# Fifth group's preparation moved half a unit and more back, and head 13 loaded in half rows and transposed by VectorE

## The chip, the core and the metric

The kernel runs on one core of a Trainium2 chip. Its engines are TensorE (PE; the weight loads of its matmuls are listed apart as PEld), VectorE (DVE), ScalarE (ACT), GpSimd (POOL) and SyncE (SP), which here only issues transfers. Each takes its instructions in program order and waits on semaphores for what the others produce. DMA transfers are issued from SP and from POOL and run on 16 DMA engines. The metric is the device time of one launch in microseconds, as the median of several runs.

## What is computed

Routed attention over 4 batches and 8 heads of 768 tokens with 64 dimensions each, and then a gated feed-forward layer (512 to 1536 and back) on the 3072 rows that come out. A query sees only the keys whose nearest of 16 centroids is the same as its own:

```python
q_assign = np.argmax(np.einsum('bhsd,hcd->bhsc', q_n, c_n), axis=-1)
k_assign = np.argmax(np.einsum('bhsd,hcd->bhsc', k_n, c_n), axis=-1)
mask = q_assign[:, :, :, None] == k_assign[:, :, None, :]
scores = np.where(mask, scale * np.matmul(q, k.transpose(0, 1, 3, 2)), -1e9)
attn = softmax(scores); x = attn @ v          # rows of all heads side by side
xn = x / sqrt(mean(x * x) + 1e-6) * rms_g
out = (silu(xn @ w_gate) * (xn @ w_val)) @ w_out
```

## The kernel before

**Units and groups.** A unit is half a batch's queries (384) for all 8 heads; there are 8 units, u = 0 to 7, and units 2b and 2b+1 belong to batch b. A group is four heads of one batch; there are 8 groups, g = 0 to 7, and head n (0 to 31) of the whole job lies in group n // 4. Units 4 and 5 use groups 4 and 5: group 4, "the fifth", is first needed at the start of unit 4, group 5 in its middle.

**What a unit does.** `attention` walks through 24 gaps, three for each head. In each gap TensorE makes two score matmuls (`s`, L348), ScalarE takes their exponential into `pT` (L352), and once per head TensorE multiplies the head before by its values into `acc` (`pv`, L366). After each pair of heads VectorE divides by the sums (`inv` L371, `x` L373), and that frees the one `acc` buffer. The mask is not applied as a mask: a one-hot of the cluster, 16 rows long, is put under the 64 rows of each transposed query and key (`qext`, `kext`), scaled so that other clusters vanish in the exponential.

**What fills the gaps.** `attention` also takes a list `fill` of pairs of a weight and a piece of work, and hands them out so that the sum of weights keeps step with the gaps. For u of 2 and more, and g = u + 2, the list is: the last 8 of the 24 gate and value parts (`gv`, L444) of the feed-forward layer of unit u-2; `rms(u-1)`, the norm of the unit before; some loads of queries and keys; the 9 output parts `o` of unit u-2 (`out_mm`, L469: 4 matmuls, three parts to a tile of 128 rows, the third followed by a copy on ScalarE and a store from SP, L473); and the first 16 gate and value parts of unit u-1. Between the last two kinds the preparation of group g is spread: `rows`, and then `clusters`.

**The preparation of a group** (`group_work`). For each head: `trans` of the queries and of the keys; then `both`, which casts both halves of the queries and one half of the keys (`cast`, L240), casts the head's v (`vcast`, L243) and issues from SP the v load of head n+4 and the query and key loads of head n+6 (`others`); then a cast of the other half of the keys. These are the 16 `rows`. `clusters` are: the products with the centroids (`sc`, L254; 16 matmuls), on VectorE a transpose, a maximum, a comparison and a transpose back for queries and keys each (L257, L262, L266, L286, with a scaling at L285 for the keys), and 16 small DMAs issued from POOL that put the one-hots under `qext` and `kext` (`place`, L297).

**Two kinds of head.** For n < BH = 14 a head is loaded with one DMA of 192 KB for the queries and one for the keys (L88), TensorE transposes it in float32 (`tq`, L221), and ScalarE or VectorE evicts it (L227, L225); the key casts are VectorE's. For n of 14 and more it is loaded in half rows of 32 floats, four DMAs of 48 KB each for queries and for keys (L96), so that VectorE's transpose in blocks of 32 (L217) gives the same layout with no TensorE and no PSUM; the key casts are POOL's. In unit 1, group 3 (heads 12 to 15) is prepared after group 2's cluster steps; heads 12 and 13 are of the first kind there. Its casts on POOL have the three loads of `wo` woven in (`load_o`, L207, with a cast from float32 in the transfer). `second_batch`, in unit 0, issues the loads of heads 12 and 13 and of v8 to v11.

**Loads held back.** LATE lists heads whose query and key loads are not issued in `others` but in a unit's fill after `rms`: 19, 20 and 21 in unit 2, 24 and 25 in unit 3, 28 and 29 in unit 4. `rms` ends with a transposing DMA from SP (L406) that makes `xnT`, which the gate and value parts of the same unit read.

**Buffers that matter.** Six staging buffers hold queries and keys (a load of head n waits until head n-6 is transposed), eight hold v, three hold pairs of transposed heads (`qkT`), and three PSUM banks (`ps_g`) serve all of `gen`: gate, val, o, sc and tq.

Of the kernel before, what the change touches and what calls it, by code (L numbers as in the profile page):

```python
# [22 lines left out]
def kernel(  # L23
# [13 lines left out]
    B, H, S, D = q.shape  # L37
# [7 lines left out]
    HG = 4  # L45
# [8 lines left out]
    CUT = 2 * FC - 8  # L54
    LEAD = 6
    NQ, NV = 6, 8
    AV = 4
    LATE = [19] + [n for n in range(20, B * H) if n % HG < 2]
    BH = 14
    BG = BH // HG  # L60

    ctx.enter_context(tc.manual_schedule())
# [17 lines left out]
    def src(a, n):  # L80
        b, h = divmod(n, H)
        return a[b, h].rearrange("(p t) d -> p t d", t=ST)

    def load(n, part, on=None):
        if n not in staged:
            staged[n] = stage.tile([P, 2, ST, D], F32, tag="qk", name="qk")
        if n < BH:
            (on or nc.sync).dma_start(out=staged[n][:, part], in_=src((q, k)[part], n))  # L88
            return

        to = staged[n][:, part].rearrange("p t d -> p (t d)").rearrange("p (i r d) -> p i r d", i=HT, d=32)
        of = (q, k)[part][n // H, n % H].rearrange("(r p i e) (c d) -> e c p i r d", p=32, i=HT, e=2, d=32)
        for e in range(2):
            for c in range(2):
                r = 32 * (2 * e + c)
                nc.sync.dma_start(out=to[r:r + 32], in_=of[e, c])  # L96

    def load_qk(n):
        if n < B * H:
            load(n, 0)  # L100
            load(n, 1)

    def load_v(n, vq=None):
        if n >= B * H:
            return
        stagedv[n] = stage.tile([P, ST, D], F32, tag="vs", name="vs", bufs=NV)
        (vq or nc.sync).dma_start(out=stagedv[n], in_=src(v, n))
# [104 lines left out]
    def trans(g, h, part, on=None):  # L212
        if (g, h // 2) not in qkT:
            qkT[g, h // 2] = qk32.tile([P, 2, 2, UQ], F32, tag="qkT", name="qkT")
        qk = staged[g * HG + h]
        if g * HG + h >= BH:
            nc.vector.transpose(qkT[g, h // 2][:, h % 2, part], qk[:, part].rearrange("p t d -> p (t d)"))  # L217
            return
        ps = ps_g.tile([P, UQ], F32, tag="gen", name="tq")
        for i in range(HT):  # L220
            nc.tensor.transpose(ps[:, i * P:(i + 1) * P], qk[:, part, 2 * i:2 * i + 2].rearrange("p t d -> p (t d)"),  # L221
                                ident_f)
        to, by = qkT[g, h // 2][:, h % 2, part], 1.0 / ZS if part and g < BG else 1.0
        if on is nc.vector:
            nc.vector.tensor_scalar_mul(to, ps, by)  # L225
        else:
            nc.scalar.activation(to, ps, ACT.Copy, scale=by)  # L227
# [5 lines left out]
    def cast(on, g, h, part, es=(0, 1)):  # L233
        for e in es:
            to = cols((kext if part else qext)[g % 4][:D, h], g, e)
            of = qkT[g, h // 2][e * D:(e + 1) * D, h % 2, part]
            if on is nc.scalar:
                nc.scalar.copy(to, of)
            else:
                on.tensor_copy(to, of)  # L240

    def vcast(n):
        nc.gpsimd.tensor_copy(vbf[n // HG % 4][:, n % HG, :, :D], stagedv[n])  # L243
# [24 lines left out]
    def cluster_steps(g, m):  # L268

        of = {}  # L270

        def products():
            of["cl"] = cluster_products(g, [(h, m) for h in range(HG)])

        def most():
            of["mx"] = largest(of["cl"])

        def same():
            of["ohT"] = asg.tile([P, UQ], BF16, tag="ohT", name="ohT", bufs=2)
            compare(of["ohT"].rearrange("p (b e c) -> p b e c", e=2, c=NC), of["cl"], of["mx"])  # L280

        def back():
            put[g, m] = asg.tile([P, UQ], BF16, tag="oh", name="oh", bufs=3)
            if m and g >= BG:
                nc.vector.tensor_scalar_mul(of["ohT"], of["ohT"], ZS)  # L285
            nc.vector.transpose(put[g, m], of["ohT"])  # L286

        return [products, most, same, back]
# [3 lines left out]
    def place(on, g, m, es=(0, 1)):  # L292

        ext = (kext if m else qext)[g % 4]
        for h in range(HG):
            for e in es:
                on.dma_start(out=ext[D:D + NC, h, e * UQ:(e + 1) * UQ],  # L297
                             in_=put[g, m][32 * h + e * NC:32 * h + (e + 1) * NC])
# [190 lines left out]
    def group_work(g):  # L489

        t, c = [], []
        for h in range(HG):
            n = g * HG + h
            w = 0.0 if n >= BH else 0.3
            t += [(w, lambda h=h: trans(g, h, 0)), (w, lambda h=h: trans(g, h, 1))]

            def others(n=n):
                vcast(n)
                load_v(n + AV)
                if n + NQ not in LATE:  # L500
                    load_qk(n + NQ)

            def both(h=h, f=others):
                cast(nc.gpsimd, g, h, 0)
                f()
                cast(nc.gpsimd if g * HG + h >= BH else nc.vector, g, h, 1, (0,))
            if g == 2:
                c.append((0.0, others))
            else:
                c += [(0.0, both), (0.0, lambda h=h: cast(nc.gpsimd if g * HG + h >= BH else nc.vector, g, h, 1, (1,)))]  # L510
        a = []
        for m in range(2):
            a += [(0.0 if i else 0.7, f) for i, f in enumerate(cluster_steps(g, m))]
            if g == 3:
                a.append((0.0, lambda m=m: place(nc.gpsimd, g, m)))
            elif g == 2:
                a.append((0.0, (lambda: (place(nc.gpsimd, g, 1), place(nc.gpsimd, g, 0, (1,)))) if m else
                          (lambda: place(nc.gpsimd, g, 0, (0,)))))
        if g > 3:
            a[:1] = [(1.4, lambda f=(a[0][1], a.pop(4)[1]): [x() for x in f])]  # L520
            a.append((0.0, lambda: [place(nc.gpsimd, g, m) for m in range(2)]))
        return t, c, a
# [12 lines left out]
    def spread(a, b):  # L535

        if not a:
            return list(b)
        w, n = [], 0
        for i, x in enumerate(a):  # L540
            w.append(x)
            while n < len(b) * (i + 1) // len(a):
                w.append(b[n])
                n += 1
        return w

    def ffn_work(u):
        n = UNITS[u][2] / HT
        return [(0.64 * n, lambda f=f, val=val: gv(u, f, val)) for f in range(FC) for val in (False, True)]

    def out_work(u):
        return [(0.86, lambda t=t, p=p: out_mm(u, t, p)) for t in range(UNITS[u][2]) for p in range(3)]
# [127 lines left out]
    for u in range(1, NU):  # L680
        ffn, o, g = ffn_work(u - 1), out_work(u - 2) if u > 1 else [], u + 2
        if u == 1:
            t, c, a = group_work(2)
            t3, c3, a3 = group_work(3)
            n = LEAD - 4
            o3 = [(0.0, lambda i=i: load_o(i)) for i in range(0, FC, 4)]
            prep = c + a + spread(weave(t3[n:], c3), o3) + a3[:5]
            idle = const.tile([P, 1], BF16)

            def norm():  # L690
                rms(0)
                nc.gpsimd.tensor_copy(idle, xn[0][:, CC - 1, HT - 1, P - 1:])
                for h in range(HG):
                    casts(pool_, H + h, K0, Q0, K1, Q1)

            hooks = {(1, 0, 0): late[6], (1, 0, 1): lambda: (late[7](), norm())}
            hooks.update({(1, *divmod(2 + i, HT)): t3[i][1] for i in range(n)})
            hooks[1, *divmod(LEAD - 1, HT)] = lambda: xtrans_all(0)
            fill = spread(ffn[:CUT], prep)
            attention([(1, h) for h in range(H)], fill, LEAD, hooks)  # L700
        else:
            fill = ffn_work(u - 2)[CUT:]
            if u == 2:
                fill = fill[:1] + spread(fill[1:], [(0.0, f) for _, f in a3[5:]])
            fill.append((0.0, lambda u=u: rms(u - 1)))
            rows, clusters = group(g)
            fill += [(0.0, lambda n=n: load_qk(n)) for n in LATE if n - n % HG == (u + 3) * HG or (u, n) == (2, 19)]
            n = 12 if u == 2 else len(rows)
            fill += spread(o, rows[:n]) + spread(ffn[:CUT], [(0.0, f) for _, f in rows[n:]] + clusters)
            attention([(u, h) for h in range(H)], fill, 1 if g < NG else 0, ahead=1)  # L710
    rest = ffn_work(NU - 2)[CUT:]
    rest[0][1]()
# [39 lines left out]
```

## Time and profile before

| | us |
|---|---|
| median of five runs | 328.94 |
| the five runs | 328.22 to 329.5 |
| the profiled execution | 329.44 |
| its span in the trace | 327.7 |
| VectorE busy, of 7.94 us from 104.34 to 112.28 (last gate and value parts, unit 3) | 5.51 |
| the same, of 7.37 us from 112.28 to 119.65 (output parts, unit 3) | 6.47 |
| DMA share from 28 to 44 us, and from 61 to 78 us | 1.29 and 1.09 |

The page gives for each engine the time that it was busy and its share of the span. A group is all instructions of one line, engine, operation and tile, as "out<-in", with the count, the total and the mean. The waits list who stood idle until whom: total, times, longest. A timeline row has start, duration, engine, line, operation, tiles, count, and in brackets the idle time before it with what ended it. The chain of waits follows the execution back from its last instruction to what released each step. A DMA share of 1 is 16 engines all busy[...].

### The profile page before, as it was taken

The page shows a single profiled execution, that of the slowest core. Times are in us where ns is not written, and L with a number is a line of the kernel's source. Part 1 is how long each engine was busy: PE and PEld are TensorE (multiplying, and loading weights), DVE is VectorE, ACT ScalarE, POOL GpSimd, SP SyncE. Part 2 cuts the span into 40 slices and gives each one's busy share as a digit, 9 for nine tenths or more (in the row PEclk, how much of TensorE's full clock was granted, in tenths as well). Part 3 has the DMA queues.
Part 4 walks back from the last instruction along what each step waited for, and adds up shares of the span by engine and source line. Part 5 has one row for each costly group of instructions (what it writes and reads, how often), then busy time and mean ns, then how long its engine had stood idle before and what let it go on. Part 6 is the DMA issues. An engine that isn't in the chain of part 4 may idle for free.

```text
span 327.7 us, 7794 instructions
## 1 busy us (share of the span) xinstructions
PE 318.7 (97%) x2851; PEld 191.4 (58%) x2865; DVE 222.8 (68%) x509; ACT 245.8 (75%) x425; POOL 137.6 (42%) x277
## 2 busy tenths in 40 slices
PE   8999899998999999999999999999999999999996
PEld 4546656654556555665566555665566656655654
DVE  6999978879378785877678694876265644685430
ACT  5899988976778867897778877798779868863322
POOL 5999499985935356450926347350000000000000
PEclk9999999999999999999999999999999999999999
DMA  7999995797546644561646540000700040001002
GB/s 261 331 268 259 239 156 103 128 184 166 91 71 159 139 88 72 117 153 60 103 85 132 142 114 34 6 21 1 146 3 0 2 112 34 0 2 74 25 1 96
DMA packets 88742, 34.24 MB, mean 104 GB/s; under 512 B 70400, under 2 KB 85632, under 8 KB 88704
## 3 DMA queue, kind: packets, MB, share of 16 engines
q1 hardware_dynamic: 79536, 27.45, 35.2%
q0 software_dynamic: 8880, 5.91, 11.1%
q8 instruction: 22, 0.36, 0.5%
q10 hardware_dynamic: 288, 0.39, 0.4%
q14 instruction: 16, 0.13, 0.1%
HBM read 28.61 MB, written 6.29 MB: 107 GB/s over the span
## 4 chain that ended last, share of the span: by engine, by line
PE 78%; DVE 9%; POOL 4%; DMA 4%; ACT 2%; issue 2%; DVEq 0%; ACTq 0%
PE o L469 18%; PE gate L444 17%; PE val L444 16%; PE s L348 15%; PE acc L366 8%; DMA wo<-in_moe_w_out_dram 3%; PE sc L254 2%; POOL qext L240 1%; POOL kext L297 1%; DVE kext L332 1%; DVE qext L332 1%; DVE pads L327 1%; DMA boot<-in_centroids_dram 1%; DVE x L373 1%; PE o L480 1%
## 5 line engine op out<-in xcount | busy, mean ns | idle before, releaser
L352 ACT ACTIVATE pT<-s,off 128x768 bf16<-128x768 f32 x192 | 170.9, 904 | 30.9 <-PE s L348 30.2
L348 PE MATMUL s<-qext,kext 80*128 80x384 bf16 x384 | 94.8, 327 | 1.5 <-ACT pT L352 0.8
L444 PE MATMUL gate<-xnT,wg 128*128 128x384 bf16 x384 | 78.3, 325 | 0.1
L444 PE MATMUL val<-xnT,wv 128*128 128x384 bf16 x384 | 78.1, 326 | 0.0
L453 DVE SCALAR_TENSOR_TENSOR th<-th,gate 128x384 f32<-128x384 f32 x84 | 46.2, 551 | 34.8 <-ACT th L452 34.2
L469 PE MATMUL o<-wo,gvT 128*128 128x512 bf16 x262 | 66.3, 378 | 2.0 <-DMA wo<-in_moe_w_out_dram 1.3
L348 PEld LDWEIGHTS <-kext 80*128 80x128 bf16 x384 | 36.4, 98 | 35.0 <-issue 7.4
L452 ACT ACTIVATE th<-gate 128x384 f32<-128x384 f32 x84 | 41.2, 490 | 15.3 <-PE gate L444 14.5
L457 DVE SCALAR_TENSOR_TENSOR gvT<-th,val 128x384 bf16<-128x384 f32 x84 | 46.2, 550 | 9.3 <-PE val L444 3.4
L444 PEld LDWEIGHTS <-wg 128*128 128x128 bf16 x384 | 36.1, 97 | 23.4 <-issue 0.8
L366 PEld LDWEIGHTS <-pT 128*128 128x128 bf16 x1152 | 43.4, 97 | 10.1 <-DVE x L373 1.1
L444 PEld LDWEIGHTS <-wv 128*128 128x128 bf16 x384 | 35.6, 97 | 22.5 <-issue 0.6
L240 POOL CAST qext<-qkT 64x384 bf16<-64x384 f32 x64 | 35.3, 557 | 29.6 <-DVE inv L371 17.5
L366 PE MATMUL acc<-vbf,pT 128*128 128x65 bf16 x1152 | 45.7, 193 | 0.6 <-ACT pT L352 0.2
L469 PEld LDWEIGHTS <-gvT 128*128 128x128 bf16 x276 | 25.9, 97 | 26.9 <-issue 1.4
L297 POOL DMA_DIRECT2D qext<-oh x48 | 23.1, 492 | 33.9 <-DVE oh L286 29.2
L240 POOL CAST kext<-qkT 64x384 bf16<-64x384 f32 x58 | 31.4, 542 | 4.4 <-DVE qkT L225 2.5
L297 POOL DMA_DIRECT2D kext<-oh x48 | 23.1, 488 | 8.3 <-DVE oh L286 7.1
L472 ACT COPY o_sb<-o 128x512 f32<-128x512 f32 x23 | 13.5, 585 | 17.3 <-PE o L469 17.3
L371 DVE RECIPROCAL inv<-acc 128x6 f32<-128x6 f32 x32 | 6.0, 188 | 25.1 <-PE acc L366 24.7
L373 DVE TENSOR_TENSOR x<-acc,inv 128x384 f32<-128x384 f32 x32 | 17.8, 558 | 1.1
L217 DVE STREAM_TRANSPOSE qkT<-qk 128x384 f32<-128x384 f32 x36 | 18.1, 550 | 0.0
(83 smaller groups left out, 228.7 us busy)
## 6 DMA issues: line engine op xcount, KB each, us to landing
vs<-in_v_dram SPq DMA_DIRECT2D x32, 192.0 KB, 4.4
out_dram<-o_sb SPq DMA_DIRECT2D x23, 256.0 KB, 2.5
qk<-in_q_dram SPq DMA_DIRECT2D x72, 48.0 KB, 2.8
qk<-in_k_dram SPq DMA_DIRECT2D x72, 48.0 KB, 2.5
qk<-in_q_dram SPq DMA_DIRECT2D x14, 192.0 KB, 4.9
qk<-in_k_dram SPq DMA_DIRECT2D x12, 192.0 KB, 5.1
wg<-in_moe_w_gate_dram POOLq DMA_DIRECT2D x4, 384.0 KB, 8.0
wv<-in_moe_w_val_dram POOLq DMA_DIRECT2D x4, 384.0 KB, 9.6
```

What stands on the lines that cost most here:

```text
L217: nc.vector.transpose(qkT[g, h // 2][:, h % 2, part], qk[:, part].rearrange("p t d -> p (t d)"))
L240: on.tensor_copy(to, of)
L297: on.dma_start(out=ext[D:D + NC, h, e * UQ:(e + 1) * UQ], in_=put[g, m][32 * h + e * NC:32 * h + (e + 1) * NC])
L348: nc.tensor.matmul(ps[:, j, :w] if nt == HT else flat[:, j * w:(j + 1) * w], lhsT=cols(kext[g % 4][:KR, hh], g, kc // HT, kc % HT * P, (kc ...
L352: nc.scalar.activation(pT[u, h][:, n * i:n * i + n, :w], of, ACT.Exp, bias=off, scale=scale if g >= BG else scale * ZS)
L366: nc.tensor.matmul(acc[:, h % 2, t], lhsT=pT[u, h][:, kc, t * P:(t + 1) * P], rhs=vbf[g % 4][:, hh, kc % HT * 2 + kc // HT], start=kc == 0 ...
L373: nc.vector.tensor_tensor(dst, acc[:, :, :nt, :D], inv[:, :, :nt].unsqueeze(3).broadcast_to([P, 2, nt, D]), op=ALU.mult)
L444: nc.tensor.matmul(ps, lhsT=w[:, c, f * P:(f + 1) * P], rhs=xnT[u][:, c, :n], start=c == 0, stop=c == CC - 1)
L452: nc.scalar.activation(th, ps, ACT.Tanh, scale=0.5)
L453: nc.vector.scalar_tensor_tensor(th, th, 1.0, ps, op0=ALU.add, op1=ALU.mult)
L457: nc.vector.scalar_tensor_tensor(gvT[u][:, f, :n], gates[u], 0.5, ps, op0=ALU.mult, op1=ALU.mult)
L469: nc.tensor.matmul(outs[u], lhsT=gvT[u][:, f, t * P:(t + 1) * P], rhs=wo[:, f], start=f == 0, stop=f == FC - 1)
```

## The change

BH becomes 13: head 13 joins the heads that are loaded in half rows and transposed by VectorE, so its key casts go to POOL, and its two transposes have weight 0 in the fill. (BG, 13 // 4, stays 3, so the scaling of the groups is as it was.) LATE becomes a table by unit: unit 2 loads heads 17, 18, 19, 20 and 21, unit 3 loads 23, 24 and 25, unit 4 loads 28 and 29. So heads 17 and 18 are no longer loaded in unit 1, nor head 23 in unit 2's rows.

In unit 2 all 16 rows of group 4 go between the first 16 gate and value parts (before: 12 between the output parts and 4 after). Its cluster steps leave unit 2 and go between the last 8 gate and value parts at the beginning of unit 3, before `rms(2)`. In unit 3, 12 rows of group 5 stay between the output parts, and 4 go with its cluster steps between the next 16 parts (before: all 16 between the output parts).

```diff
-    LATE = [19] + [n for n in range(20, B * H) if n % HG < 2]
-    BH = 14
+    LATE = {2: (17, 18, 19, 20, 21), 3: (23, 24, 25), 4: (28, 29)}
+    BH = 13
...
-                if n + NQ not in LATE:
+                if not any(n + NQ in x for x in LATE.values()):
                     load_qk(n + NQ)
...
             fill = ffn_work(u - 2)[CUT:]
-            if u == 2:
-                fill = fill[:1] + spread(fill[1:], [(0.0, f) for _, f in a3[5:]])
+            if u in (2, 3):
+                fill = fill[:1] + spread(fill[1:], [(0.0, f) for _, f in a3[5:]] if u == 2 else c4)
             fill.append((0.0, lambda u=u: rms(u - 1)))
             rows, clusters = group(g)
-            fill += [(0.0, lambda n=n: load_qk(n)) for n in LATE if n - n % HG == (u + 3) * HG or (u, n) == (2, 19)]
-            n = 12 if u == 2 else len(rows)
-            fill += spread(o, rows[:n]) + spread(ffn[:CUT], [(0.0, f) for _, f in rows[n:]] + clusters)
+            fill += [(0.0, lambda n=n: load_qk(n)) for n in LATE.get(u, ())]
+            rows = [(0.0, f) for _, f in rows]
+            if u == 2:
+                fill += o + spread(ffn[:CUT], rows)
+                c4 = clusters
+            else:
+                n = 12 if u == 3 else len(rows)
+                fill += spread(o, rows[:n]) + spread(ffn[:CUT], rows[n:] + clusters)
```

`a3[5:]` are the cluster steps of group 3's keys, which were and stay in unit 2's beginning. `spread(a, b)` lays the items of b evenly between those of a.

## The prediction

> **What bounds it.** First the busy row of the page, then TensorE's waits, then its timeline where they fall.
>
> ```profile
> PE 318.7 (97%) x2851; PEld 191.4 (58%) x2865; DVE 222.8 (68%) x509; ACT 245.8 (75%) x425; POOL 137.6 (42%) x277
> ...
> PE o L469 <- DMA wo<-in_moe_w_out_dram: 1.3, 1, 1.3
> ```
>
> TensorE is busy for 318.7 of 327.7 us, and from 45 us on it stands still once for more than half a microsecond. So an edit is worth what it takes off TensorE's own work, plus what it does to waits like that one. The chain of waits between 68 and 79 us shows what it hangs on:
>
> ```profile
> 68.82 0.45 POOL kext L240
> 69.27 8.74 DMA wo<-in_moe_w_out_dram
> 78.01 0.04 issue
> 78.05 1.02 PE o L469 x4
> ```
>
> Backwards from there the chain is POOL work end to end to 53.45: the third wo load is issued when POOL has got through its casts. Three loads, asked one by one (columns: KB, us from issue to landing), took:
>
> ```profile
> wo<-in_moe_w_out_dram POOLq DMA_DIRECT2D x1, 512.0 KB, 6.3
> ...
> wo<-in_moe_w_out_dram POOLq DMA_DIRECT2D x1, 512.0 KB, 8.1
> ...
> wo<-in_moe_w_out_dram POOLq DMA_DIRECT2D x1, 512.0 KB, 8.7
> ```
>
> The second and third ran beside head 18's loads and three v loads (SP, 63.50 to 73.65); the windows there show a DMA share of 1.1 to 1.3[...].
>
> **Head 13 off TensorE.** Its transposes are these, in unit 1:
>
> ```profile
> 51.74 0.51 PE L348 MATMUL s<-qext,kext 80*128 80x384 bf16 x2
> 52.08 0.49 PE L221 MATMUL tq<-ident_f,qk 128*128 128x128 f32 x3
> 52.41 0.81 PE L444 MATMUL val<-xnT,wv 128*128 128x384 bf16 x4
> 53.06 0.50 PE L348 MATMUL s<-qext,kext 80*128 80x384 bf16 x2
> 53.65 0.55 PE L221 MATMUL tq<-ident_f,qk 128*128 128x128 f32 x3
> 54.04 0.81 PE L444 MATMUL gate<-xnT,wg 128*128 128x384 bf16 x4
> ```
>
> The first set costs 52.41 - 52.08 = 0.33. A score pair holds TensorE 0.34, so the second takes 54.04 - 53.40 = 0.64, its wait with it. Gain 0.97 us, on the path. ScalarE loses two evictions of 0.49. VectorE gains two transposes (0.57) and gives two casts (0.34 and 0.41) to POOL: +0.4 us in a stretch where it idles 0.46 and 0.35 us at 55 and 58. Bounds: 0 to 0.3 us of TensorE; I take 0. By my pacing of the fill with the new weights (two of 0.3 become 0) no item of unit 1 changes its gap.
>
> POOL gets those two casts, 0.53 each by its spacing there, ahead of the second and third wo loads: the third is issued at 69.27 + 1.06 = 70.33.
>
> Head 13's load becomes 8 DMAs of 48 KB for 2 of 192 KB, at 28.7 us, ahead of v8 to v12 and heads 14 to 16 on SP. [...] By the rows: from 79 to 98 us nearly only such loads ran.
>
> ```profile
> q1 hardware_dynamic: 10582, 1.50, 48.3%
> ```
>
> 0.483 x 19 us x 16 engines over 10582 packets is 13.9 ns each, so 3072 packets take 2.7 us of all engines, against 1.1 us for 393 KB at the 357 GB/s of 5 to 10 us. [...] costs 1.6 us of transfer, and at most 8 x 1.2 = 9.6 us of SP time at the pace of head 14's loads (33.5 to 43.1). What waits: POOL's v casts at 49.09 (v11 lands near 38.5 now, 47 at worst) and head 15's transposes at 59 (its loads land at 52.6 now, 54 to 56 after). Either fits: cost 0, with an upper bound of 1 us.
>
> **Loads of heads 17 and 18 out of unit 1.** That is 16 SP DMAs less between 57 and 70 us, and v16 to v19 follow v15 at about 58 to 60. The third wo load is then alone but for the second, issued 3.9 us ahead. TensorE wants it at 76.78 - 0.97 = 75.8 (the pacing keeps this output part in gap 7). By the nearest row, the first load, 6.3 us with head 17's tail beside it: it lands at 76.6, a wait of 0.8. [...] I take 5.8 us, the row less some contention: a wait of 0.3 stays of 1.27. Gain 0.97; bounds 0.47 and 1.27.
>
> **Fifth group later.** In unit 2 eight transposes, casts and v casts move from the output parts to the next gate and value parts. VectorE's load there is no denser, since the cluster steps leave. The five heads of LATE are 40 DMAs on SP, from 79.8 us. At the 0.70 us that 24 of them took in the trace (80.76 to 97.61), heads 17, 18 and 19 land some 2 us or more before their transposes at about 90, 95 and 99.
>
> Then unit 3. Its first eight gate and value parts get the cluster steps: 1.43 us of TensorE that comes out of unit 2, and nine VectorE instructions, 4.8 us by their rows. Today's stretch:
>
> ```profile
> 112.28 1.03 PE L469 MATMUL o<-wo,gvT 128*128 128x512 bf16 x3
> ...
> 119.65 0.71 PE L366 MATMUL acc<-vbf,pT 128*128 128x65 bf16 x18
> ```
>
> ```profile
> 113.68 0.16 DVE L400 SCALAR_TENSOR_TENSOR ms<-ss 128x3 f32<-128x3 f32 x1 [0.45 <-ACT xn L393]
> ...
> 118.14 0.56 DVE L373 TENSOR_TENSOR x<-acc,inv 128x384 f32<-128x384 f32 x1
> ```
>
> VectorE begins the norm 1.40 us after the first output part, and idles 2.5 us before it. With about 22 instructions queued at 0.48 each and waits on ScalarE between them, I reckon the norm 2.15 us after it. From its first instruction to the end of x took 80.13 - 75.13 = 5.0 us in unit 2, less one transpose 4.5: x is free at 6.65. The next acc matmuls want it at 7.37 today; the pacing puts the first output part one gap later and the acc stays in its gap, one output part and one score pair (1.20) sooner: 6.17. A wait of 0.5 us, bounds 0 and 1.2. Behind it nothing is late: POOL's 16 placing DMAs (7.8 us) end near 117, when the sixth group's casts start.
>
> **SP ahead of the xn transpose of unit 3.** SP is past five heads, three output stores, head 22 and four v loads at 83.5 + 48i, with i the time of one half-row DMA: 117.1 at 0.70. The norm ends near 116.7. The transpose lands 3.8 to 4.9 later, 121 to 122; the first gate of unit 3 wants it at 122.9 (124.32 less 1.94 plus 0.5). Cost 0, slack 1 us. Head 23, loaded after it, lands by 126.4 for a transpose at 126.7.
>
> **Sum.** -0.97 - 0.97 + 0.5 = -1.44 us. That stands against the profiled execution, 329.44 (327.7 span and 1.74 around it), as 328.0; that run was one of the longest shown, and against the median, 328.94, it is **327.5**.
>
> **Rivals.**
> 1. All covers hold: no wo wait, no acc wait: -0.97 - 1.27 = -2.24, 326.7. For it: [...] 2.5 us of idle VectorE before the norm. Against: 6.3 us is the fastest wo load seen.
> 2. The wo wait stays. Its load is 1.06 later on POOL and wanted 0.97 sooner, so it must get 2.03 us faster to break even on the wait itself. At 7.2 us (between 6.3 and 8.1) it lands at 77.5, a wait of 1.7: -0.97 + 0.45 + 0.5 = 0, 328.9. For it: the second wo load still runs ahead in the same queue. Against: 16 half-row loads and the v loads are gone from its side.
> 3. Slower: SP's queue takes over. Five heads stand in one run ahead of the transposed xn of unit 3. Each 0.01 us of i costs 0.48. It decides from i = 0.73; 0.76 eats the gain, 0.78 makes it slower by 0.3%. At 0.81, what head 23's eight took from 105.34 to 111.80, the sum is about 331. For it: such paces occur. Against: the mean over the other seven heads loaded from 80.76 to 137.34 is 0.705, and head 23's load could also be waiting for its buffer.
>
> **Chances.** The forecast 0.42 (326.9 to 328.1 by its own bounds), rival 1 0.16, rival 2 0.24, rival 3 0.18. Differences under 0.3%, about 1.0 us, can't be told from none here, so faster means below 327.95: nearly all of the first two, 0.55; same 0.28, most of rival 2 and the forecast's upper edge; slower 0.17. The range is 326.4 (rival 1 less the runs' spread) to 329.9 (rival 2 plus its bounds, with the mild end of rival 3).
>
> **What would show it.** TensorE's transposes drop by 6 to 78; wo's largest landing falls below 6.5 us and TensorE's wait on it to 0.3 or less; a wait of acc on x near 0.5 us appears in unit 3; VectorE's norm starts about 2 us after the output parts there. I am wrong if wo still takes 7 us or more, if gate of unit 3 waits for the transposed xn, or if VectorE waits for head 15's, 19's or 23's load.

## The result, and the profile after

The changed kernel takes **329.75 us** (median of 29 runs, 328.45 to 332.38) against 328.52 for the kernel before on the same chip (50 runs, 327.59 to 330.51): a ratio of 1.0037 [1.0026, 1.0048]. It is slower by 0.37%, where faster by about 0.4% was forecast. The time lies inside the range, but only because the upper end of the range had room for rivals 2 and 3. A run more than 1.5% above the fastest of its kernel is left out of the medians and ratios here and below; that concerns two runs of e3 and one of e10.

The profiled execution was one of the longest, 332.1 us with a span of 330.3. First the busy row of its page, then TensorE's waits (us in total, times, longest).

```profile
PE 319.4 (97%) x2845; PEld 191.2 (58%) x2859; DVE 221.2 (67%) x509; ACT 245.3 (74%) x423; POOL 138.6 (42%) x279
```

```profile
PE o L469 <- DMA wo<-in_moe_w_out_dram: 2.4, 1, 2.4
...
PE acc L366 <- DVE x L373: 0.5, 2, 0.4
```

TensorE has six instructions fewer and yet is busy 0.7 us longer, and the wait for `wo` has nearly doubled instead of going. TensorE's timeline shows both, and the new wait on `x` in unit 3:

```profile
75.11 0.71 PE L366 MATMUL acc<-vbf,pT 128*128 128x65 bf16 x18
78.19 1.02 PE L469 MATMUL o<-wo,gvT 128*128 128x512 bf16 x4 [2.36 <-DMA wo<-in_moe_w_out_dram]
...
79.37 1.86 PE L469 MATMUL o<-wo,gvT 128*128 128x512 bf16 x4
81.03 0.85 PE L348 MATMUL s<-qext,kext 80*128 80x384 bf16 x2
81.67 1.61 PE L469 MATMUL o<-wo,gvT 128*128 128x512 bf16 x4
...
121.15 0.71 PE L366 MATMUL acc<-vbf,pT 128*128 128x65 bf16 x18 [0.38 <-DVE x L373]
```

TensorE wanted the output part at 78.19 - 2.36 = 75.83. After the wait, four matmuls that took 1.03 us before (first row below) take 1.86 and 1.61, and a pair of scores 0.85 for 0.49. The windows of the changed kernel give the reason (the last three columns: granted clock, DMA share, GB/s):

```profile
79.24 1.03 PE L469 MATMUL o<-wo,gvT 128*128 128x512 bf16 x4
```

```profile
76.00:77.00 1.00, 0.00 (x0) 0.00 (x0) 0.82 (x6) 0.21 (x1) 0.00 (x0) 1.00 0.14 26
77.00:78.00 1.00, 0.00 (x0) 0.00 (x0) 1.00 (x2) 0.00 (x0) 0.00 (x0) 1.00 0.07 14
...
79.00:80.00 1.00, 1.00 (x5) 0.45 (x4) 0.64 (x2) 0.76 (x2) 1.00 (x3) 0.71 0.13 30
80.00:81.00 1.00, 1.00 (x3) 0.30 (x2) 0.00 (x0) 0.63 (x1) 1.00 (x3) 0.50 0.53 90
81.00:82.00 1.00, 1.00 (x4) 0.45 (x3) 0.00 (x0) 0.03 (x1) 1.00 (x3) 0.50 1.14 83
82.00:83.00 1.00, 1.00 (x4) 0.40 (x3) 0.00 (x0) 0.87 (x1) 0.76 (x2) 0.58 1.26 290
```

Two things are to be seen. In the last two microseconds of the load the DMA share is 0.14 and 0.07, as much as two engines of sixteen and then one would make (an estimate: 16 x 0.14 = 2.2 and 16 x 0.07 = 1.1; the profile doesn't show the engines singly). And 1.2 us after TensorE has started again its clock falls to a half; by the rows it stays there for 0.58 + 1 + 1 + 0.84 = 3.42 us, and 79.37 to 83.11 takes 3.74 us for work that takes 2.05 at full clock: 1.7 us lost.

The chain of waits has the third `wo` load (issue, us to landing) as

```profile
70.61 7.53 DMA wo<-in_moe_w_out_dram
```

issued 0.28 later than predicted, and 1.7 us longer than the 5.8 taken.

The sum for this execution: -0.96 from 54 us on (head 13), +1.09 at `wo`, +1.67 for the clock: 1.80, and the first gate of unit 2 starts at 88.97 against 87.16. The first gate of unit 3 starts at 126.68 against 124.32, so 0.55 more came in between (the wait on `x` is 0.38 of it). From there to the end the distance grows by only 0.2.

**But this execution isn't typical.** The mean clock of each run tells of such a loss: 3.42 us at half clock is 0.5% of the run, and 0.995 is what the profile shows. Of the changed kernel's other 29 runs none lies below 0.998. What made the median 1.2 us longer has to be something other than the lost clock.

### The profile page after: what moved, and what is told of

It is laid out like the page before. It is cut to its first block, busy times and chain, and to the rows that moved or that the text cites. A ratio compares the mean times of both kernels' runs of the same rounds, so it can differ in the third digit from the quotient of the medians.

```text
span 330.3 us, 7787 instructions
## 1 busy us (share of the span) xinstructions
PE 319.4 (97%) x2845; PEld 191.2 (58%) x2859; DVE 221.2 (67%) x509; ACT 245.3 (74%) x423; POOL 138.6 (42%) x279
## 4 chain that ended last, share of the span: by engine, by line
PE 77%; DVE 8%; DMA 6%; POOL 2%; ACT 2%; issue 2%; SPq 2%; DVEq 0%; ACTq 0%
PE gate L444 17%; PE o L469 16%; PE val L444 16%; PE s L348 15%; PE acc L366 8%; DMA qk<-in_k_dram 3%; DMA wo<-in_moe_w_out_dram 2%; PE sc L254 2%; SPq L96 2%; DVE xn L403 1%; POOL qext L240 1%; DVE pads L327 1%; DMA boot<-in_centroids_dram 1%; DVE kext L332 1%; DVE qext L332 1%
## 5 line engine op out<-in xcount | busy, mean ns | idle before, releaser
L469 PE MATMUL o<-wo,gvT 128*128 128x512 bf16 x262 | 67.4, 385 | 3.1 <-DMA wo<-in_moe_w_out_dram 2.4
L240 POOL CAST kext<-qkT 64x384 bf16<-64x384 f32 x60 | 32.4, 540 | 4.5 <-DVE qkT L225 2.5
L217 DVE STREAM_TRANSPOSE qkT<-qk 128x384 f32<-128x384 f32 x38 | 19.7, 553 | 0.2 <-DMA qk<-in_k_dram 0.2
```

What stands on the lines that cost most here:

```text
L469: nc.tensor.matmul(outs[u], lhsT=gvT[u][:, f, t * P:(t + 1) * P], rhs=wo[:, f], start=f == 0, stop=f == FC - 1)
```

## The experiments

"Before" is the median of the kernel before, run beside it on the same chip; its four values in the table belong to four chips. The ratio is estimated over all runs with its 95% interval, and needn't be the quotient of the two medians. Diffs are against the changed kernel, unless they say otherwise.

| | what | us (runs) | before | ratio |
|---|---|---|---|---|
| a0 | the changed kernel again | 330.02 (10) | 328.86 | 1.0031 [1.0016, 1.0047] |
| e3 | before, with head 13's part alone | 331.35 (16) | 328.86 | 1.0061 [1.0037, 1.0086] |
| e4 | the fifth group's part alone | 330.57 (6) | 328.86 | 1.0066 [1.0040, 1.0091] |
| e1 | changed, `wo` loads first | 330.02 (9) | 328.86 | 1.0047 [1.0027, 1.0067] |
| e2 | before, `wo` loads first | 328.10 (16) | 328.94 | 0.9973 [0.9966, 0.9981] |
| e8 | changed, v21 to v23 later on SP | 330.19 (9) | 328.94 | 1.0039 [1.0025, 1.0054] |
| e10 | e1 and e8 | 329.26 (15) | 328.94 | 1.0011 [0.9997, 1.0024] |
| e9 | e10, and an earlier norm in unit 3 | 329.33 (14) | 328.94 | 1.0005 [0.9993, 1.0016] |
| e11 | e1, head 17 loaded in unit 1 again | 328.39 (14) | 328.52 | 0.9994 [0.9981, 1.0007] |
| e12 | e11, and an earlier norm in unit 3 | 327.73 (22) | 328.52 | 0.9970 [0.9961, 0.9980] |
| e13 | e2 with head 13's part | 329.60 (20) | 328.52 | 1.0032 [1.0013, 1.0051] |
| e14 | changed, head 17 loaded in unit 1 again | 332.15 (7) | 328.76 | 1.0104 [1.0066, 1.0142] |

### The changed kernel again (a0)

Nothing is edited; this gives a second profile, of a run of ordinary length.

> The changed kernel once more, for a second trace. Theory W (the third wo load is the loss): TensorE again waits more than 1.3 us for wo at the first tile's third output part, and about 0.4 us for x in unit 3; where the wait is long, the granted clock falls for some us behind it. Rival S (the first trace was an odd one and the loss is spread over many small waits): the wo wait is under 1 us and the time is 1.2 us over the kernel before all the same.

Its span is 328.4, and TensorE's waits have changed places:

```profile
PE gate L444 <- DMA xnT<-xn: 1.2, 1, 1.2
...
PE o L469 <- DMA wo<-in_moe_w_out_dram: 0.6, 1, 0.6
PE acc L366 <- DVE x L373: 0.6, 2, 0.4
```

The third `wo` load, issued at 70.89, took 5.75 us here, the clock stayed at 1.00, and the first gate of unit 2 comes at 85.80, 1.36 us sooner than before. All of it and more is lost by the first gate of unit 3, at 124.84 against 124.32:

```profile
124.84 0.81 PE L444 MATMUL gate<-xnT,wg 128*128 128x384 bf16 x4 [1.18 <-DMA xnT<-xn]
```

SP's timeline shows how (first a0, then before):

```profile
111.70 2.84 SPq L96 DMA_DIRECT2D qk<-in_q_dram  x4
114.58 2.63 SPq L96 DMA_DIRECT2D qk<-in_k_dram  x4
117.30 1.51 SPq L107 DMA_DIRECT2D vs<-in_v_dram  x3
118.98 1.32 SPq L406 DMA_TRANSPOSE xnT<-xn  x1
```

```profile
112.56 0.88 SPq L107 DMA_DIRECT2D vs<-in_v_dram  x2
117.68 1.49 SPq L406 DMA_TRANSPOSE xnT<-xn  x1
```

Before, SP had nothing to issue for four microseconds ahead of the transposing DMA and took it up when the norm ended. In a0 the norm ended at 115.14 + 2.08 = 117.22, but SP, which has issued loads and stores end to end since 81.03, gets to it at 118.98: 1.76 us late. That run of loads began behind unit 2's transpose, which SP issued no sooner than before, because VectorE's norm there waits for ScalarE (two rows of a0, then one of before):

```profile
75.41 0.16 DVE L400 SCALAR_TENSOR_TENSOR ms<-ss 128x3 f32<-128x3 f32 x1 [0.87 <-ACT xn L393]
79.42 1.55 SPq L406 DMA_TRANSPOSE xnT<-xn  x1
```

```profile
79.12 1.58 SPq L406 DMA_TRANSPOSE xnT<-xn  x1
```

Unit 3's transpose then lands in 5.82 us instead of the 3.8 of before. The v loads issued just ahead of it look like the reason, but e11 will show that they aren't. In the profile of the long run the same queue did no harm: there the longer wait and the lost clock had put the norm 3.2 us later, and SP was ready (it took the transpose up at 120.54, 0.14 after the norm). **The two losses hide each other**: in these two profiles, the one with the long `wo` wait has no wait for `xnT`.

### Each part alone (e3, e4)

For e3, against the kernel before:

```diff
-    BH = 14
+    BH = 13
```

For e4:

```diff
-    BH = 13
+    BH = 14
```

> Kernel before, with head 13 in half rows and on VectorE alone; heads 17 and 18 and the fifth group as they were. Theory W: POOL gets to the third wo load some 1.1 us later and TensorE wants it 0.96 sooner, beside the same loads, so the wo wait is 2.5 to 3.5 us, and this half alone is slower than before by 0.5 to 3 us, the clock included. Rival G (the fifth group's move is the loss): faster by about 1 us.

> Changed kernel with head 13 as before (whole rows, TensorE, its key casts on VectorE); the later loads and the fifth group's move stay. Theory W: the third wo load is issued near 69.4 and lands 7.2 to 7.5 later, near 76.8, when TensorE wants it: a wait of 0 to 0.3, and with the acc wait of 0.55 the time is 0.5 us under the kernel before. Rival G: slower than before by 0.5 us or more.

Both are slower, and neither is the cause alone. With head 13 alone the third `wo` load took 7.27 us from its issue at 73.13 and nothing waits for `xnT`:

```profile
80.44 1.02 PE L469 MATMUL o<-wo,gvT 128*128 128x512 bf16 x4 [2.12 <-DMA wo<-in_moe_w_out_dram]
```

The clock stayed at 1.00 in this execution, but all 18 runs spread from 328.68 to 334.26, and in 8 of them the mean clock is 0.995 or less, so a clock loss like the one above is common there. With the fifth group alone the waits are 0.6 for `wo`, 0.5 for `xnT` and 0.5 for `x`. Both profiles also show a start some 2.5 us slower, by 18 us, in instructions that the edits don't touch: TensorE's first transposes and centroid products between 5.5 and 10.5 us took up to 1.8 times as long as in the other profiles (six transposes 1.49 us for 0.82). So their spans can't be compared with the others, only their waits.

### The three `wo` loads ahead of unit 1's preparation (e1, e2)

```diff
-            prep = c + a + spread(weave(t3[n:], c3), o3) + a3[:5]
+            prep = c + a + o3 + weave(t3[n:], c3) + a3[:5]
```

> Changed kernel, with the three wo loads issued together before the fourth group's casts. Theory W: the wo wait is gone and no clock is lost; what is left against the kernel before is -0.96 (transposes), -1.27 (its own wo wait) and +0.55 (acc), so 326.8 or 0.995. Rival L (the half-row loads and the later fifth group cost time by themselves, on DMA, SP or VectorE): no wo wait, and still 328.5 or more.

> Kernel before, with the three wo loads issued together before the fourth group's casts and nothing else. Theory W (what the wo wait is worth in the kernel before): no wait for wo, 0.5 to 1.3 us faster than before, 327.3 to 328.2. Rival: the wo wait only moves, because the earlier loads hold up those of heads 16 to 18 or the cluster rows behind them on POOL: no faster.

The loads are issued from 59 to 62 us in both, take longer (9.0 and 9.3 us in the median) and nobody waits for them. In the kernel before this gains 0.84 us. In the changed one it gains nothing, for what is won at `wo` is lost at the transposed `xn` (the step of e1's chain of waits, then TensorE's timeline):

```profile
118.70 5.80 DMA xnT<-xn
```

```profile
124.55 0.81 PE L444 MATMUL gate<-xnT,wg 128*128 128x384 bf16 x4 [1.49 <-DMA xnT<-xn]
```

The norm ended 0.6 us sooner than in a0 and SP came 0.28 sooner: it is SP's queue, not the norm, that sets the gate.

### Room on SP by order alone (e8, e10, e9)

v21 to v23, which are issued just ahead of the transposing DMA, go behind it; e10 adds `wo` first; e9 also moves the second half of the fifth group's cluster steps behind the norm, so that the norm is earlier on VectorE.

```diff
+    VLATE = (21, 22, 23)
...
-                load_v(n + AV)
+                if n + AV not in VLATE:
+                    load_v(n + AV)
...
             fill += [(0.0, lambda n=n: load_qk(n)) for n in LATE.get(u, ())]
+            fill += [(0.0, lambda n=n: load_v(n)) for n in VLATE if u == 3]
```

In e9 also:

```diff
-                fill = fill[:1] + spread(fill[1:], [(0.0, f) for _, f in a3[5:]] if u == 2 else c4)
+                fill = fill[:1] + spread(fill[1:], [(0.0, f) for _, f in a3[5:]] if u == 2 else c4[:4])
...
-                fill += spread(o, rows[:n]) + spread(ffn[:CUT], rows[n:] + clusters)
+                fill += spread(o, (c4[4:] if u == 3 else []) + rows[:n]) + spread(ffn[:CUT], rows[n:] + clusters)
```

> Changed kernel with one edit: the loads of v21, v22 and v23 are issued from SP behind the transpose of xn of unit 3 and not ahead of it. Theory Q (SP's queue: what stands ahead of that transpose sets its start, and bulk loads issued just before it its landing): SP takes the transpose up within 0.3 us of the end of the norm and it lands in 4.5 us or less, so unit 3's first gate doesn't wait for it; where the wo wait is short the time falls by about 1.2 us against the changed kernel, to 328.5. Rival N (the transpose is late because VectorE's norm is late): the wait for it stays over 1 us and the time stays 329.7 or more.

> Changed kernel with the wo loads first and v21 to v23 behind the transpose. Theories W and Q together: neither wait, only the acc wait of 0.4 to 0.6 us is left of the new ones: about 327.7, 1 us under the kernel before. Rival N: a wait for the transpose over 1 us, 329 or more.

> As the last one, and the second half of the fifth group's cluster steps goes behind the norm of unit 2, between the output parts of unit 3. Theory: VectorE begins the norm at least 1 us earlier against the output parts, acc no longer waits for x, and the time falls by 0.5 us more, to about 327.2. Rival: the steps behind the norm hold x up as much, and nothing is gained.

e8 does away with the wait for `xnT`, and the time stays. SP takes the transpose up 0.56 us after the norm; it lands in 5.4 us, where 4.5 or less was expected with the v loads behind it. VectorE's timeline shows who is late in its place (lines are one higher in this kernel):

```profile
122.37 0.58 DVE L218 STREAM_TRANSPOSE qkT<-qk 128x384 f32<-128x384 f32 x1 [1.89 <-DMA qk<-in_k_dram]
...
127.37 0.58 DVE L218 STREAM_TRANSPOSE qkT<-qk 128x384 f32<-128x384 f32 x1 [1.04 <-DMA qk<-in_q_dram]
...
130.10 0.58 DVE L218 STREAM_TRANSPOSE qkT<-qk 128x384 f32<-128x384 f32 x1 [1.71 <-DMA qk<-in_k_dram]
```

VectorE stands in its own order before the transposes of heads 22 and 23, whose loads come late on SP; the `gvT` behind it comes late, and `gate` waits 1.5 us for that. With `wo` first as well (e10) 1.0 us of that wait is left, and with the earlier norm (e9) 0.5 and another 0.6 on `th`. These two are no longer clearly slower than before, but not faster either.

### Less on SP behind unit 2's norm (e11, e12, e14)

The loads of head 17 go back to unit 1, so four late heads instead of five stand in unit 2. e11 has `wo` first, e12 the earlier norm as well (e9's second diff, without the v loads' move), e14 neither.

```diff
-    LATE = {2: (17, 18, 19, 20, 21), 3: (23, 24, 25), 4: (28, 29)}
+    LATE = {2: (18, 19, 20, 21), 3: (23, 24, 25), 4: (28, 29)}
```

> Changed kernel with the wo loads first, and head 17 loaded in unit 1 again, as before the change, so that four heads and not five stand on SP in unit 2. Theory Q (SP's queue between the two transposes of xn is past its capacity): eight DMAs of 0.66 to 0.7 us less, so SP is idle for 2 us or more ahead of the transpose of unit 3, no gate waits for it, and head 23 is there in time; the acc wait of 0.55 stays. 1.2 to 1.5 us under the same kernel with head 17 late (330.0), so 328.5 to 328.8 or less. Rival A (the fifth group's rows and steps on VectorE are the loss, whatever SP does): 329.5 or more.

> As the last one, with the second half of the fifth group's cluster steps behind the norm of unit 2. Theory: with SP relieved, the earlier norm is worth the acc wait, 0.5 us under the last one. Rival: as with the full queue, nothing.

> Changed kernel with head 17 loaded in unit 1 again and nothing else: the wo loads stay where they were. With the changed kernel (both late), wo first (330.0) and wo first with head 17 back (328.4) this makes the square. If the two waits stand in a row (W and Q): the wo wait is back at 0.6 us or more, the wait for the transposed xn stays away, and the time is 328.4 plus that wait, 329.0 to 330. If SP's queue alone was the loss: 328.4, whatever wo does.

With eight DMAs fewer SP is through its v loads at 113.2 and waits for the norm, as before the change (e12):

```profile
111.71 1.51 SPq L107 DMA_DIRECT2D vs<-in_v_dram  x3
116.31 1.33 SPq L406 DMA_TRANSPOSE xnT<-xn  x1
```

No gate waits for `xnT` in either. In e11 SP stands idle for 5.2 us between the v loads and the transpose, and still the transpose takes 5.9 us to land (last row: count, us to landing):

```profile
111.48 1.51 SPq L107 DMA_DIRECT2D vs<-in_v_dram  x3
118.19 1.34 SPq L406 DMA_TRANSPOSE xnT<-xn  x1
```

```profile
xnT<-xn SPq DMA_TRANSPOSE x1, 5.9
```

So the late start comes from SP's queue, but the long landing does not come from the v loads ahead of it. e11 differs from e1 by that head alone; they ran on two chips, but their ratios to before, 0.9994 and 1.0047, don't overlap in their intervals. (e11's profile is of its longest run, 329.60.) e12 is faster than before by 0.3%; its first gate of unit 3 comes at 122.45, 1.87 sooner than before. e11 still has a wait of 0.85 us for a one-hot placed under `kext`, at 83.68, which e12 has not; e12's further edit comes after that point in time, so only the wait on `x` in unit 3 (0.38, gone) can be put down to the edit, and the rest of the 0.66 us between them stays unexplained. And e12 is no faster than e2, which only puts the `wo` loads first in the kernel before: 0.9970 [0.9961, 0.9980] and 0.9973 [0.9966, 0.9981], on two chips. What head 13 and the later fifth group add to that one line is not seen in the time, though TensorE has 0.96 us less to do.

e14 is the fourth case: the same head back in unit 1, but `wo` not first. It is the slowest of all, over 2 us slower than the 329 to 330 expected, which left the clock out. Its wait and its windows:

```profile
PE o L469 <- DMA wo<-in_moe_w_out_dram: 3.5, 1, 3.5
```

```profile
78.00:79.00 1.00, 0.00 (x0) 0.00 (x0) 0.99 (x3) 0.00 (x0) 0.00 (x0) 0.95 0.10 20
79.00:80.00 1.00, 0.79 (x2) 0.25 (x2) 0.56 (x1) 0.00 (x0) 0.53 (x2) 0.50 0.01 2
80.00:81.00 1.00, 1.00 (x4) 0.42 (x3) 0.00 (x0) 0.00 (x0) 1.00 (x3) 0.50 1.47 135
81.00:82.00 1.00, 1.00 (x5) 0.38 (x4) 0.00 (x0) 0.84 (x2) 1.00 (x3) 0.50 1.28 12
82.00:83.00 1.00, 1.00 (x6) 0.44 (x5) 0.00 (x0) 0.65 (x1) 1.00 (x3) 0.84 0.42 86
```

The third `wo` load, issued at 70.53, took 8.64 us. Head 17's loads were issued up to 69.55 and four v loads, held back behind them, from 69.65 to 71.63; in a0 the v loads were out by 63.65. TensorE stood for 3.47 us and then ran at half clock; the mean clock is 0.995 in six of the seven runs. So the two places pull against each other: head 17's loads in unit 1, with the v loads behind them, lengthen the `wo` load, and in unit 2 they fill SP ahead of the transpose. Either loss alone undoes the gain; of the four cases only the one with `wo` first and head 17 in unit 1 is free of both.

### Head 13 with no `wo` wait in the way (e13)

Against e2:

```diff
-    BH = 14
+    BH = 13
```

> Kernel before with the wo loads first and head 13 in half rows and on VectorE; the loads and the fifth group stay where they were. Theory W: head 13 alone lost only through the wo load; with that out of the way its 0.96 us of TensorE are a gain, so 0.8 to 1.0 us under the kernel before with the wo loads first (328.1): 327.1 to 327.3. Rival D (the half-row load of head 13 in the crowded stretch of unit 0 and 1 costs time by itself): 328.1 or more.

If half rows for head 13 cost nothing on SP, as predicted, this should be the fastest: e2 less 0.97. It is 0.3% slower than before. SP's timeline, and TensorE's:

```profile
80.82 1.51 SPq L107 DMA_DIRECT2D vs<-in_v_dram  x3
82.50 1.55 SPq L406 DMA_TRANSPOSE xnT<-xn  x1
```

```profile
86.86 0.81 PE L444 MATMUL gate<-xnT,wg 128*128 128x384 bf16 x4 [1.89 <-DMA xnT<-xn]
```

The norm of unit 2 ended at 78.05, but SP had issued loads almost without a gap from 28.7 us on and took its transpose up at 82.50. In e2 the norm ended at 79.58 and SP came at 80.49: already late, but no gate waited. The six DMAs more come 50 us ahead of the place where they are paid for. (The runs of e13 spread from 327.60 to 332.01, so other losses than this one take part.)

## Why the prediction was wrong

- **Head 13 off TensorE: right.** Predicted 0.97, measured 0.96, TensorE's instructions fewer by six.
- **Its half rows, "cost 0": wrong in kind.** Nobody waited for v11 or head 15, the two that the prediction names. The cost is the queue's time: six DMAs more on SP, which are paid at the next transfer that SP has to issue at once. In the change this stays hidden, since heads 17 and 18 leave unit 1; e13 shows it bare, 1.89 us.
- **The `wo` term, "5.8 us, a wait of 0.3 stays": the size was off.** 5.75 us and 0.58 in one execution, 7.53 us and 2.36 in the other of the same kernel. The first is the size that was taken, an estimate of the author's from the 6.3 us of the first load before; the second lies within rival 2. Both loads were issued 0.3 to 0.6 later than reckoned. The half clock behind the 2.36 us wait was not foreseen at all; it cost 1.7 us in that execution, the only one of the changed kernel's first 30 with a mean clock below 0.998.
- **The fifth group's cluster steps in unit 3: right.** The norm began 116.59 - 114.43 = 2.16 us after the output part (predicted 2.15), and 0.55 us were lost (predicted 0.5), 0.38 of it as the wait itself.
- **"SP ahead of the xn transpose of unit 3: cost 0, slack 1 us": this is the step that failed.** SP was to be free at 117.1; in a0 it was at 118.9. The pace was nearly as assumed (40 DMAs from 81.03 to 109.5 and head 22's eight in 5.5 us: 0.708). But the queue started at 81.03, not 79.8: the prediction let unit 2's norm come a microsecond sooner with TensorE, while VectorE's norm waits for ScalarE there (0.87 us at 75.41) and its transpose was issued at 79.42, no sooner than before (79.12). The stores and v loads took 0.3 more than reckoned. Then the landing, 5.8 us where 3.8 to 4.9 was taken from the trace of before. At 4.9 the wait would have been 0.3 instead of 1.2. The start is put down to the queue by e1, e11 and e12; what lengthens the landing stays open (last section).
- **Rival 3 was the right one**, but its point of decision, a pace of 0.73, was not: it was worked out with the early start and the short landing, and the pace reached only 0.71. Over 48 DMAs, 0.03 of pace is 1.4 us; the later start (1.2) and the longer landing (0.9 to 2.0) came to more than that.
- **The sum.** For a0 against the profile of before: -0.96 for head 13, -0.69 at `wo`, +0.3 for a start that was later by as much (first score pair at 10.98 for 10.66), then +1.18 for `xnT`, +0.38 for `x` and 0.3 in small pieces: +0.5 at the first gate of unit 3, and 0.7 in the spans, where -1.44 was predicted. Of the 2.1 us between, the `xnT` wait, put at nothing, is 1.18, and the `wo` wait 0.28. The profile of before was one of its longer runs (329.44, where its medians here are 328.5 to 328.9), which accounts for much of what is missing to the 1.2 us of the medians.

What stays open: why the same `wo` load takes 5.75 us in one execution and 7.53 in another, why the transpose of unit 3 lands so late, and which of the waits were short in the three fastest runs of the changed kernel (about 328.5), none of which has a profile.

## What to carry to other kernels

Count a queue that issues transfers as an engine with its own busy time, here 0.7 us for each half-row DMA: when it has no gap left, moving loads only changes who waits, and the transfer that something waits for at once pays (in a0, e1 and e13 the transpose of just-computed data: waits of 1.18, 1.49 and 1.89 us). When an edit makes one engine earlier, check whether each later start in the sum really hangs on that engine, before moving it along. And two waits in a row can hide each other, so an edit that removes one is best tried together with one that removes the other: `wo` first gained nothing and head 17 back lost 0.7% more, but both together gained 0.4% over the changed kernel, and with the earlier norm the result is faster than before. But try the smallest edit by itself too: `wo` first alone, in the kernel before, was as fast.

## What was not expected of the hardware

- After TensorE stood for 2.36 and for 3.47 us, its clock went to a half some 3.6 and 3.2 us after it had stopped, for 3.42 us in both cases (read off the windows of 1 us). After 1.27 us, in the profile of before, and after 2.12 us, in that of e3, it stayed at full speed. What decides between the two is not shown.
- In the last two microseconds of the 7.53 us `wo` load the DMA share was 0.14 and 0.07, which by the estimate above (16 x 0.14 = 2.2, 16 x 0.07 = 1.1) is two engines of sixteen at work and then one.
- The transposing DMA of unit 3 landed 3.8 us after its issue in the profile of before and 4.7 us after it in that of e13, where the fifth group's cluster steps are in unit 2. Where they are in unit 3 it took 6.0 us in the changed kernel's profile, 5.8 in a0 and e1, 5.9 in e4 and e11, and 5.5 in e12. How long SP had been idle doesn't explain it: it took 5.9 us after 5.2 idle us in e11. POOL's 16 small DMAs for the one-hots come shortly before it or beside it there (in the changed kernel's profile they are issued from 113.88 to 121.49 and the transpose at 120.54; in that of before none is issued from 116 to 122), which was not tested; it can't be the only reason, since the changed kernel's transpose at 232.12 took 5.3 us, and POOL's last small DMA had been issued at 222.0.
- In two of the profiles, e3's and e4's, the same instructions were about 2.5 us later by 18 us, and in e3 still were at 78 us. TensorE's instructions from 5.5 to 10.5 us took up to 1.8 times as long (six transposes 1.49 us for 0.82 in e3), though the mean granted clock of both executions is 1.0; why is open.
